# Stores and reloads moved from SyncE's DMA queue to GpSimd's, a spare buffer for one weight chunk, and another order at the first rows and the last stores

## The chip, the cores and the metric

One Trainium2 chip (trn2), one core, one launch. The metric is the device time of that launch in microseconds (us). The engines are named as in the profile: PE (TensorE matmul), PEld (its weight loads), DVE (VectorE), ACT (ScalarE), POOL (GpSimd) and SP (SyncE, which here only issues DMAs). Each engine runs its own instruction list in order; semaphores tie the lists together. A DMA is issued by one engine's list (its "queue") and runs on 16 shared DMA engines. If an issue has to wait for a semaphore, everything behind it in that list waits too.

## The reference, cut to what matters

```python
def reference(A_x, A_dft_seq_re, A_dft_seq_im, A_dft_hid_re, A_dft_hid_im, B_x, B_w1, B_b1, B_w2, B_b2):
    x = A_x                                  # (1, 2048, 640), f32
    xn = _layernorm(x, axis=-1)
    # fourier half: y = Cr @ (xn @ Wr^T) - Ci @ (xn @ Wi^T), sequence 2048, hidden 640
    # MLP half:     gelu(xn @ w1 + b1) @ w2 + b2, w1 (640, 1536), w2 (1536, 640)
    return x + _A_ref(xn, A_dft_seq_re, A_dft_seq_im, A_dft_hid_re, A_dft_hid_im) + _B_ref(xn, B_w1, B_b1, B_w2, B_b2)
```

B_x is not used: both halves work on the same normalized rows.

## The kernel before

All matmuls are f32 by way of a split: each operand is kept as a rounded high part (`high`, ACT, L182) and the rest (`low`, DVE, L185), and a product is three matmuls, high by high, high by low, low by high (`product`, L307 to L309; `hidden`, L325).

The 2048 rows are four blocks of 512 (t = 0 to 3). The first third of the time is the MLP half, the rest the Fourier half; only the first third, the beginning and the end bear on the change.

**Beginning.** Four chunks of 128 rows of block 0 are loaded, two by SP and two by ACT (`load_x`, L204). PE runs 26 matmuls on zeros meanwhile (`NWARM`, L662). DVE takes mean and variance of each chunk (`ln_stats`, L211 and L212), `ln_scale` makes the factors, and the normalized chunks are transposed on PE.

**Block 0** goes through 12 hidden units (`hidden`, then `gelu`, then `output`) while `background(i)` brings in other rows: block 2's (`rows_b`) and block 1's (`row`) are normalized in place (L227), stored to a DRAM tensor `xs` (`put_rows`, L232) and loaded back in a layout for transposing (`load_z`, L262: four loads, `z_b` for block 2, `row` for block 1). DVE transposes these (L266), and ACT and DVE split them into the moving operands of the next stage.

**Blocks 1 and 2** run together in `pair(k)`, k = 0 to 5: each pair makes two hidden units of both blocks out of seven products (`window`) in place of eight. The units of block 1 are used at once; those of block 2 are stored to DRAM (`keep`, `gs`, L851) out of a tile `ab` of which there are two. The weights of a pair are made from two w1 chunks by `make_pieces`; chunks are loaded by `load_w1` (L285, four DMAs each) into three buffers `w1r`, the next two when the two of a pair are used up (after "Cl" and "Dl"). `w2r`, also three buffers, holds w2 chunks in block 0's stage, later other tiles. Beside the pairs, called by `beside_pair(k, at)` at numbered points of a pair (in the order 2, 5, 6, 3, 7, 4):

- `finish`: ACT adds the bias to an output bank, DVE transposes it (L384), POOL adds it to `xo` (L386); then `store_sums` writes `xo` to DRAM (`ys`, L864, three stores).
- `by_chunks` copies 512 rows of `xs` to `xn` in DRAM (L860).
- `prep_w(j, 0..2)`: the DFT matrices of the hidden axis are combined, split into the staging tile `wst` (which lies where `xo` was, so it waits for the `ys` stores) and other small tiles, and stored (`wit`, L438).

After the pairs block 2's units are loaded back (`load_unit`, L931) for its outputs; block 3's rows are normalized, stored, loaded back (`z`) and transposed in `between(p)`; block 3 then runs like block 0.

**Fourier half.** The DFT along the sequence, with combined forms of both matrices; its last products are transposed on DVE, added and stored (`store`, L1152; last lines L1581 to L1591).

Order of the work: `manual_schedule`, so each engine's list is in the order of the calls. In the kernel before SP issues all DMAs but the first rows, the first two w1 chunks and some of the last stores, which ACT issues.

Of the kernel before, what the change touches and what calls it, by code (L numbers as in the profile page):

```python
# [10 lines left out]
F32 = mybir.dt.float32  # L11
# [4 lines left out]
P = 128  # L16
Q = 4
B = 32
EPS = 1e-5
NWARM = 26  # L20
# [5 lines left out]
def kernel(  # L26
# [204 lines left out]
    def put_rows(c):  # L231
        nc.sync.dma_start(xs[c * P : (c + 1) * P], xt[c])  # L232
# [25 lines left out]
    def load_z(z, t):  # L258

        v = rows_of(xs, t)  # L260
        for q in range(Q):
            nc.sync.dma_start(z[q * B : (q + 1) * B], v[:, :, q * DQ : (q + 1) * DQ])  # L262
# [13 lines left out]
    def load_w1(i, eng=nc.sync):  # L276
# [4 lines left out]
        t = early.tile([P, ND, P], F32, tag="w1r", bufs=3, name=f"w1r{i}")  # L281
# [126 lines left out]
    def put_w(w, j, main, odd=None, negative=False):  # L408
# [28 lines left out]
        for t, c0, c1 in parts:  # L437
            nc.sync.dma_start(wits[w][j][:, :, c0:c1], t.bitcast(F32))  # L438
# [209 lines left out]
    warm = early.tile([P, TB], F32R, tag="w1r", bufs=3, name="warm")  # L648
    for c in range(NC):
        load_x(c, (nc.sync, nc.scalar)[c % 2])  # L650
# [3 lines left out]
    nc.vector.tensor_copy(warm, zeros)  # L654

    nc.scalar.activation(eps[:, 1:2], eps[:, 0:1], AF.Sqrt)
    load_w1(0, nc.scalar)
    load_w1(1, nc.scalar)

    wacc = bank(5)  # L660
    for k in range(NWARM):
        nc.tensor.matmul(wacc, warm[:, :P], warm, start=True, stop=True)  # L662
# [19 lines left out]
    for c in range(NC):  # L682
        ln_stats(c)

    last = NC - 1
    nc.vector.tensor_scalar(MV[:, last, 5:6], MV[:, last, 0:1], -1.0, None, op0=ALU.mult)
    ln_scale(NC)
# [4 lines left out]
        bias=MV[:, last, 5:6],  # L692
    )
    nc.scalar.activation(xp[:, last], xp[:, last], AF.Copy, scale=MV[:, last, 3:4])
    for c in (0, 1, last, 2):
# [114 lines left out]

    def make_pieces(k, *what):
# [6 lines left out]
        for w in what:  # L818
# [14 lines left out]
            if w in ("Cl", "Dl"):  # L833
                load_w1(n + 3 + (w == "Dl"))
# [15 lines left out]
    def keep(g, a):  # L850
        nc.sync.dma_start(gs[g % NF], a)  # L851
# [10 lines left out]
    def store_sums(t):  # L862
        for k, (c0, c1) in enumerate(YCOLS):
            nc.sync.dma_start(ys[k][t], xo[t][:, :, c0:c1])  # L864
# [5 lines left out]
    def beside_pair(k, at):  # L870
# [20 lines left out]
        if at == 6:  # L891
# [3 lines left out]
            turn_w(1, j)  # L895
        if at == 3:
            if k == 1:
                A["wst"] = zo_tile("wst", (P, NB * DQ), F32R)
            prep_w(j, 0)
# [6 lines left out]
        if at == 7:  # L906
            prep_w(j, 1)
            if k == LASTK:
                A["gs"] = place("xab3", (P, 5, TB), F32)
                for i in range(3, 6):  # L910
                    load_unit(i)
                prep_w(j, 2)
        if k < LASTK and at == 4:
            prep_w(j, 2)
# [708 lines left out]
```

## Time and profile before

| | us |
|---|---|
| runs | 886.62, 885.71, 883.77; median 885.71 |
| the profiled execution's own time | 888.06 |
| its span | 886.0 |
| PE busy (3718 matmuls) | 856.2 (97%) |
| DVE busy | 684.9 (77%) |
| ACT busy | 364.4 (41%) |
| POOL busy (22 instructions) | 22.8 (3%) |
| DMA: SP's queue, share of 16 engines | 70.5% |
| mean granted clock of PE | 0.989 |

How to read it: a line of a view names the kernel's line (L308), the engine, the operation, and out<-in by tile names. In brackets behind a timeline line stands the idle time of that engine just before the instruction, and what ended it. "SPq" and "ACTq" are DMA issues; the time of a DMA itself runs from its issue to its landing. The granted clock is the share of full speed that PE was given. A DMA share is the time that packets took, as a share of the time of all 16 DMA engines.

What the issues on SP cost and how long the transfers take to land, from the tile and DMA views (median ns of an issue; median us from issue to landing): xs stores 392, 4.8; z_b loads 481, 6.0; ys stores 524, 6.2; wit stores 504, 3.7; gs stores 452, 3.7.

### The profile page before, as it was taken

To read this page: it belongs to the slowest core of one execution; us is meant where nothing else is said; L and a number is where in the kernel's file an instruction comes from. 1 tells how busy PE (TensorE), PEld (TensorE's weight loads), DVE (VectorE), ACT (ScalarE), POOL (GpSimd) and SP (SyncE) were. 2 spreads that over 40 slices of the span, in tenths; PEclk is the share of its full clock that TensorE was granted. 3 is DMA by queue.
4 is the path that set the end of the run, shared out by engine and by line. 5 is a ranking of instruction groups with operands and counts; after the bars stand their busy time and mean duration, and the time that the engine had idled before them with its cause. 6 is when DMAs were issued, how large, how long until landed. Compare 5 with 4: busy or idle time off the path is not lost.

```text
span 886.0 us, 10517 instructions
## 1 busy us (share of the span) xinstructions
PE 856.2 (97%) x3718; PEld 701.0 (79%) x3718; DVE 684.9 (77%) x892; ACT 364.4 (41%) x520; POOL 22.8 (3%) x22
## 2 busy tenths in 40 slices
PE   8998979999889999999999999999999999999997
PEld 6886857878668788888888888888888888888885
DVE  6866957775674568898989888888977988886586
ACT  5554555554424455543343434332232423323241
POOL 0000011000030300000000000000000000000000
PEclk9998999999999999999999999999999999999999
DMA  6986448998989697896865259946475779904364
GB/s 178 308 228 162 95 102 217 282 277 265 293 250 199 162 365 281 150 182 161 196 141 161 56 149 325 249 95 178 114 178 189 226 210 217 333 18 172 119 179 88
DMA packets 228547, 171.76 MB, mean 194 GB/s; under 512 B 83728, under 2 KB 198416, under 8 KB 227856
## 3 DMA queue, kind: packets, MB, share of 16 engines
q1 hardware_dynamic: 222544, 169.13, 70.5%
q10 hardware_dynamic: 5952, 1.97, 0.9%
q8 instruction: 29, 0.48, 0.2%
q14 instruction: 22, 0.18, 0.1%
HBM read 124.92 MB, written 51.38 MB: 199 GB/s over the span
## 4 chain that ended last, share of the span: by engine, by line
PE 74%; DMA 12%; DVE 6%; SPq 3%; ACT 2%; issue 1%; POOL 1%; DVEq 0%; ACTq 0%; POOLq 0%
PE banks L308 23%; PE banks L307 23%; PE banks L309 23%; PE banks L325 5%; DMA gs<-ab 2%; DMA w1r<-in_B_w_dram 1%; DMA xs<-row 1%; DMA row<-in_A_x_dram 1%; DMA wit<-wst 1%; DVE hs L185 1%; DMA xn<-xs 1%; SPq L285 1%; PE banks L662 1%; SPq L398 1%; DMA ys<-xo 1%
## 5 line engine op out<-in xcount | busy, mean ns | idle before, releaser
L308 PE MATMUL banks<-as,xab 128*128 128x512 f32 x407 | 158.5, 389 | 0.0
L309 PE MATMUL banks<-as,xab 128*128 128x512 f32 x407 | 158.4, 389 | 0.0
L307 PE MATMUL banks<-as,xab 128*128 128x512 f32 x407 | 158.4, 389 | 0.0
L182 ACT ACTIVATE as<-r 128x1024 fp32r<-128x1024 f32 x80 | 85.0, 1062 | 173.3 <-PE banks L309 148.5
L185 DVE TENSOR_TENSOR as<-r,as 128x1024 fp32r<-128x1024 f32 x80 | 97.2, 1216 | 38.8 <-ACT as L182 38.8
L308 PEld LDWEIGHTS banks<-as,xab 128*128 128x128 f32 x407 | 76.4, 188 | 16.4 <-DVE as L185 0.6
L307 PEld LDWEIGHTS banks<-as,xab 128*128 128x128 f32 x407 | 76.4, 188 | 16.0
L309 PEld LDWEIGHTS banks<-as,xab 128*128 128x128 f32 x407 | 76.4, 188 | 15.7
L307 PE MATMUL banks<-as,xc 128*128 128x512 f32 x224 | 87.1, 389 | 0.0
L308 PE MATMUL banks<-as,xc 128*128 128x512 f32 x224 | 87.1, 389 | 0.0
L309 PE MATMUL banks<-as,xc 128*128 128x512 f32 x224 | 87.1, 389 | 0.0
L182 ACT ACTIVATE as<-rt 128x1024 fp32r<-128x1024 f32 x32 | 34.0, 1062 | 69.8 <-PE banks L309 57.9
L185 DVE TENSOR_TENSOR hs<-ab,hs 128x512 fp32r<-128x512 f32 x36 | 26.3, 732 | 39.8 <-ACT hs L182 39.4
L325 PE MATMUL banks<-xt,xab 128*128 128x512 f32 x240 | 56.8, 390 | 0.2 <-ACT xt L182 0.2
L307 PE MATMUL banks<-hs,xc 128*128 128x512 f32 x120 | 47.9, 399 | 6.8 <-DVE ot L384 6.5
L325 PEld LDWEIGHTS banks<-xt,xab 128*128 128x128 f32 x240 | 44.7, 188 | 10.3 <-ACT xt L182 1.3
L308 PE MATMUL banks<-hs,xc 128*128 128x512 f32 x120 | 47.3, 394 | 2.0 <-DVE hs L185 2.0
L307 PEld LDWEIGHTS banks<-as,xc 128*128 128x128 f32 x224 | 42.0, 188 | 8.8
L309 PEld LDWEIGHTS banks<-as,xc 128*128 128x128 f32 x224 | 42.0, 188 | 8.7
L308 PEld LDWEIGHTS banks<-as,xc 128*128 128x128 f32 x224 | 42.0, 188 | 8.7
L309 PE MATMUL banks<-hs,xc 128*128 128x512 f32 x120 | 47.0, 391 | 0.0
L185 DVE TENSOR_TENSOR as<-rt,as 128x1024 fp32r<-128x1024 f32 x32 | 38.8, 1212 | 5.3 <-ACT as L182 5.3
(200 smaller groups left out, 1605.8 us busy)
## 6 DMA issues: line engine op xcount, KB each, us to landing
raw<-in_A_dft_seq_re_dram SPq DMA_DIRECT2D x64, 256.0 KB, 5.6
raw<-in_A_dft_seq_im_dram SPq DMA_DIRECT2D x64, 256.0 KB, 5.2
w1r<-in_B_w_dram SPq DMA_DIRECT2D x136, 80.0 KB, 3.1
wit<-wst SPq DMA_DIRECT2D x15, 384.0 KB, 5.0
ws<-wit SPq DMA_DIRECT2D x15, 384.0 KB, 5.4
xn<-xs SPq DMA_DIRECT2D x4, 1280.0 KB, 8.4
wit<-wst SPq DMA_DIRECT2D x20, 256.0 KB, 3.2
forms_ab<-xab SPq DMA_DIRECT2D x4, 1280.0 KB, 7.9
```

Source lines behind the costliest of these rows:

```text
L182: nc.scalar.activation(h, s, AF.Copy)
L185: nc.vector.tensor_tensor(l, s, h.bitcast(F32), op=ALU.subtract)
L285: eng.dma_start(t[q * B : (q + 1) * B], v[q, :, :, f0 : f0 + P])
L307: nc.tensor.matmul(acc, wh, mh, start=first, stop=False, skip_group_check=goes_on)
L308: nc.tensor.matmul(acc, wh, ml, start=False, stop=False, skip_group_check=goes_on)
L309: nc.tensor.matmul(acc, wl, mh, start=False, stop=last, skip_group_check=goes_on)
L325: nc.tensor.matmul(acc, W1[i][:, a, j * P : (j + 1) * P], XT[j][:, b], start=n == 0, stop=n == len(steps) - 1)
L398: nc.sync.dma_start(t[q * B : (q + 1) * B], v[:, :, s0 : s0 + B])
L662: nc.tensor.matmul(wacc, warm[:, :P], warm, start=True, stop=True)
```

## The change

1. `put_rows`, `load_z`, `put_w`'s stores, `keep` and `store_sums` issue on POOL's queue instead of SP's.
2. w1 chunk NF + 5 = 17 takes a `w2r` buffer, and the loads of chunks 15 to 20 are called earlier (`NEXT_W1`): 15 by pair 0's pieces "Cl", 16 and 17 by its "Dl", 18 and 19 by pair 1's, 20 by pair 2's; from 21 on as before.
3. `prep_w` of the first hidden chunk: step 0 at point 7 of pair 1 (was 3), step 1 at point 4 (was 7), step 2 at point 5 of pair 2 (was 4 of pair 1). The others keep their points.
4. First rows: SP loads all four chunks, chunk 1 first; ACT works out chunk 1's mean and variance, DVE those of the other three; chunks are transposed in the order 0, 2, 1, 3. 19 instead of 26 matmuls on zeros, in three tiles that are the three `w1r` buffers, so that the loads of w1 chunks 0, 1 and 2, now all on SP, wait for matmul 4, 8 and 19.
5. Last stores: the add `v1` of the last stage moves behind the split of the next operand (`form`); the four stores of three pieces are shared out between SP and ACT in another way, and the very last piece is transposed, added and stored whole and not in two halves.

```diff
...
 Q = 4
 B = 32
 EPS = 1e-5
-NWARM = 26
+NWARM = 19
+NGATE = 4
 TAIL = 4
 PADL = 8
 
...
             put_rows(c)
 
     def put_rows(c):
-        nc.sync.dma_start(xs[c * P : (c + 1) * P], xt[c])
+        nc.gpsimd.dma_start(xs[c * P : (c + 1) * P], xt[c])
 
     def ln_apply_chunked(dst, c):
 
...
 
         v = rows_of(xs, t)
         for q in range(Q):
-            nc.sync.dma_start(z[q * B : (q + 1) * B], v[:, :, q * DQ : (q + 1) * DQ])
+            nc.gpsimd.dma_start(z[q * B : (q + 1) * B], v[:, :, q * DQ : (q + 1) * DQ])
 
     def transpose_z(key, z, j):
         zt[key] = mr.tile([P, TB], F32, tag="zt", bufs=2, name=f"zt{key}")
...
         if i >= 3 * NF:
             return
         f0 = (i % NF if i < 2 * NF else AGAIN[i - 2 * NF]) * P
-        t = early.tile([P, ND, P], F32, tag="w1r", bufs=3, name=f"w1r{i}")
+        t = early.tile([P, ND, P], F32, tag="w2r" if i == NF + 5 else "w1r", bufs=3, name=f"w1r{i}")
         w1r[i] = t
         v = w1.rearrange("(q c i) f -> q i c f", q=Q, i=B)
         for q in range(Q):
...
             nc.scalar.activation(h, odd, AF.Copy, scale=-1.0)
             nc.vector.scalar_tensor_tensor(l, odd, -1.0, h.bitcast(F32), op0=ALU.mult, op1=ALU.subtract)
         for t, c0, c1 in parts:
-            nc.sync.dma_start(wits[w][j][:, :, c0:c1], t.bitcast(F32))
+            nc.gpsimd.dma_start(wits[w][j][:, :, c0:c1], t.bitcast(F32))
 
     def prep_w(j, k):
 
...
 
     zeros = rows.tile([P, TB], F32, tag="yt", bufs=2, name="zeros")
 
-    warm = early.tile([P, TB], F32R, tag="w1r", bufs=3, name="warm")
-    for c in range(NC):
-        load_x(c, (nc.sync, nc.scalar)[c % 2])
+    warms = [early.tile([P, TB], F32R, tag="w1r", bufs=3, name=f"warm{k}") for k in range(3)]
+
+    for c in (1, 0, 2, 3):
+        load_x(c)
     nc.gpsimd.memset(eps, EPS)
     make_identity(nc, ident)
     nc.vector.memset(zeros, 0.0)
-    nc.vector.tensor_copy(warm, zeros)
+    for warm in warms:
+        nc.vector.tensor_copy(warm, zeros)
 
     nc.scalar.activation(eps[:, 1:2], eps[:, 0:1], AF.Sqrt)
-    load_w1(0, nc.scalar)
-    load_w1(1, nc.scalar)
+    load_w1(0)
+    load_w1(1)
 
     wacc = bank(5)
     for k in range(NWARM):
+        warm = warms[min(k // NGATE, 2)]
         nc.tensor.matmul(wacc, warm[:, :P], warm, start=True, stop=True)
     load_w1(2)
     load_w2(0)
...
         for j in range(ND):
             nc.tensor.transpose(tacc[j][:, c * P : (c + 1) * P], xp[:, c, j * P : (j + 1) * P], ident)
 
-    for c in range(NC):
-        ln_stats(c)
-
-    last = NC - 1
-    nc.vector.tensor_scalar(MV[:, last, 5:6], MV[:, last, 0:1], -1.0, None, op0=ALU.mult)
-    ln_scale(NC)
+
+    last = 1
+    m = MV[:, last]
+    scratch = mr.tile([P, 2 * TB], F32, tag="hs", bufs=3, name="scratch")[:, :D]
+    nc.scalar.activation(scratch, xt[last], AF.Copy, accum_out=m[:, 4:5])
+    nc.scalar.activation(m[:, 5:6], m[:, 4:5], AF.Copy, scale=-1.0 / D)
     nc.scalar.activation(
         chunked(xp[:, last]),
         xt[last].rearrange("p (q c i) -> p q c i", q=Q, i=B),
         AF.Identity,
-        bias=MV[:, last, 5:6],
+        bias=m[:, 5:6],
     )
+    nc.scalar.activation(scratch, xp[:, last], AF.Square, accum_out=m[:, 2:3])
+    nc.scalar.activation(m[:, 1:2], m[:, 2:3], AF.Copy, scale=1.0 / D)
+    nc.scalar.activation(m[:, 0:1], m[:, 5:6], AF.Copy, scale=-1.0)
+    for c in (0, 2, 3):
+        ln_stats(c)
+    ln_scale(NC)
     nc.scalar.activation(xp[:, last], xp[:, last], AF.Copy, scale=MV[:, last, 3:4])
-    for c in (0, 1, last, 2):
+    for c in (0, 2, last, 3):
         if c != last:
             ln_apply_chunked(xp[:, c], c)
         transpose_x(c)
...
             WP[key] = w[:, lo : lo + 2 * n * P].rearrange("p (a b) -> p a b", a=2)
             lo += 2 * n * P
 
+
+    NEXT_W1 = (
+        {"Cl": (15,), "Dl": (16, 17)},
+        {"Cl": (18,), "Dl": (19,)},
+        {"Cl": (20,)},
+        {"Cl": (21,), "Dl": (22,)},
+        {"Cl": (23,), "Dl": (24,)},
+        {"Cl": (25,), "Dl": (26,)},
+    )
+
     def make_pieces(k, *what):
         if k >= NF // 2:
             return
...
                 high(dst[:, 0], src)
             else:
                 low(dst[:, 1], src, dst[:, 0])
-            if w in ("Cl", "Dl"):
-                load_w1(n + 3 + (w == "Dl"))
+            for i in NEXT_W1[k].get(w, ()):
+                load_w1(i)
 
     def window(acc, key, col, form, first, odd=None):
 
...
             output(g, (e,))
 
     def keep(g, a):
-        nc.sync.dma_start(gs[g % NF], a)
+        nc.gpsimd.dma_start(gs[g % NF], a)
 
     def finish(t, *es, home=None):
 
...
 
     def store_sums(t):
         for k, (c0, c1) in enumerate(YCOLS):
-            nc.sync.dma_start(ys[k][t], xo[t][:, :, c0:c1])
+            nc.gpsimd.dma_start(ys[k][t], xo[t][:, :, c0:c1])
 
     in_zt = {"home": mr, "tag": "zt"}
 
...
                 by_chunks(k - 1)
             turn_w(0, j)
             turn_w(1, j)
+
+        steps = {7: (0,), 4: (1,)} if k == 1 else {3: (0,), 7: (1, 2) if k == LASTK else (1,), 4: () if k == LASTK else (2,)}
+        if k == 2 and at == 5:
+            prep_w(0, 2)
         if at == 3:
-            if k == 1:
-                A["wst"] = zo_tile("wst", (P, NB * DQ), F32R)
-            prep_w(j, 0)
             if j + 1 < ND:
                 load_w(0, j + 1)
                 load_w(1, j + 1)
             if k == LASTK:
                 load_x(12)
                 load_x(13)
-        if at == 7:
-            prep_w(j, 1)
-            if k == LASTK:
-                A["gs"] = place("xab3", (P, 5, TB), F32)
-                for i in range(3, 6):
-                    load_unit(i)
-                prep_w(j, 2)
-        if k < LASTK and at == 4:
-            prep_w(j, 2)
+        if k == 1 and at == 7:
+            A["wst"] = zo_tile("wst", (P, NB * DQ), F32R)
+        for n in steps.get(at, ()):
+            prep_w(j, n)
+        if k == LASTK and at == 7:
+            A["gs"] = place("xab3", (P, 5, TB), F32)
+            for i in range(3, 6):
+                load_unit(i)
         if k == LASTK and at == 2:
             for i in range(3):
                 load_unit(i)
...
             for k in names:
                 nc.sync.dma_start(part_of(t, k), sums[t, k])
 
-    def store(t, src, c0, c1, both=False, n0=0, n1=NB):
+    def store(t, src, c0, c1, on_act=0):
 
         for q in range(Q):
-            (nc.scalar if both and q > 1 else nc.sync).dma_start(
-                rows_of(out, t)[:, n0:n1, q * DQ + c0 : q * DQ + c1], src[q * B : (q + 1) * B, n0:n1]
+            (nc.scalar if q >= Q - on_act else nc.sync).dma_start(
+                rows_of(out, t)[:, :, q * DQ + c0 : q * DQ + c1], src[q * B : (q + 1) * B]
             )
 
     def reload(lo, w, which="xab"):
...
             return f
 
         def out_b(k):
-            return lambda: store(tb, columns(k), 2 * k * B, 2 * (k + 1) * B, last and k == 1)
+            return lambda: store(tb, columns(k), 2 * k * B, 2 * (k + 1) * B, Q if last and k == 1 else 0)
 
         yb1, yb2 = in_two(0), in_two(1)
-        yb4 = to(yo[tb, 4], vs, f"yb4_{tb}", lambda: store(tb, yo[tb, 4], 4 * B, DQ, last))
+        yb4 = to(yo[tb, 4], vs, f"yb4_{tb}", lambda: store(tb, yo[tb, 4], 4 * B, DQ))
         f5s = [lambda u=u: f5(u) for u in range(2)] if not last else [lambda: None] * 2
         f6s = [lambda u=u: f6(u) for u in range(2)] if not last else [lambda: None] * 2
-        pre = {
-            17: [lambda: add(s(1, "v1"), s(1, "v1"), x_)],
-        }.get(n, [])
+        v1 = lambda: add(s(1, "v1"), s(1, "v1"), x_)
+        pre = [v1] if n == 17 and not last else []
         post = {
 
             0: [lambda: gather(1, tb, "v1", z_), lambda: gather(1, tb, "v", vs, op=ALU.subtract), f5s[0]],
...
             14: [lambda: add(s(1, "v2"), s(1, "v2"), z_), yb1],
             15: [yb1] if last else [load_yb(0)],
             16: [] if last else [load_yb(1)],
-            17: [yb2, yb2] if last else [yb1, yb2],
+            17: [v1, yb2, yb2] if last else [yb1, yb2],
             18: [yb4] if last else [yb2],
             19: [f6s[0]],
             20: [] if last else [f6s[1], yb4],
...
 
 
     t = blocks[-2][1]
-    y = yo[t]
-    add_turned(y[:, :, 2 * B : 3 * B], turned(bank(X), "yt_2"))
-    store(t, y[:, :, 2 * B : 3 * B], 2 * B, 3 * B, True)
-    yt = A["yt"]("yt_last")[:, 0].rearrange("p (n i) -> p n i", i=B)
-    d, a = y[:, :, 3 * B : 4 * B], bank(X + 1).rearrange("p (n i) -> p n i", i=B)
-    for n0 in (0, NB // 2):
-        rows_ = slice(n0, n0 + NB // 2)
-        nc.vector.transpose(yt[:, rows_], a[:, rows_])
-        add(d[:, rows_], d[:, rows_], yt[:, rows_])
-        store(t, d, 3 * B, 4 * B, True, n0, n0 + NB // 2)
+    for k, on_act in ((2, Q), (3, Q // 2)):
+        d = yo[t][:, :, k * B : (k + 1) * B]
+        add_turned(d, turned(bank(X + k - 2), f"yt_{k}"))
+        store(t, d, k * B, (k + 1) * B, on_act)
 
 
 # ---- launch: one core; inputs and outputs as the reference has them ----
```

## The prediction

> **What bounds the kernel now.** I read the page first (PE busy 97% of an 886.0 us span, so at most some 30 us are idle), then the windows of the span, then PE's waits, then the queue that the waits lead to. The windows (columns: stretch, busy PE, PEld, DVE, ACT, POOL with counts, granted clock, DMA share, GB/s):
>
> ```profile
> 0.00:13.22 13.22, 10.70 (x47) 8.55 (x47) 8.22 (x25) 4.62 (x8) 0.74 (x7) 1.00 0.56 174
> 13.22:74.50 61.28, 61.28 (x270) 50.30 (x270) 41.84 (x84) 32.29 (x48) 0.00 (x0) 1.00 0.91 252
> 74.50:82.20 7.70, 3.76 (x10) 2.54 (x9) 6.79 (x11) 5.14 (x10) 0.00 (x0) 0.74 0.45 118
> 82.20:117.70 35.50, 35.50 (x152) 29.17 (x151) 30.28 (x49) 19.22 (x33) 0.00 (x0) 0.96 0.51 111
> 117.70:145.00 27.30, 19.90 (x71) 14.59 (x70) 16.38 (x31) 13.16 (x26) 6.35 (x5) 0.87 0.51 129
> 145.00:296.00 151.00, 141.69 (x606) 113.84 (x605) 98.85 (x196) 74.96 (x147) 13.24 (x9) 0.99 0.90 248
> 296.00:879.40 583.40, 583.39 (x2571) 481.99 (x2569) 480.84 (x497) 215.01 (x253) 2.50 (x2) 1.00 0.68 185
> 879.40:886.00 6.60, 0.00 (x0) 0.00 (x0) 1.66 (x4) 0.00 (x0) 0.00 (x0) 0.83 0.44 73
> ```
>
> From 296 us to 879.4 us PE never stops, so nothing can be won there; all holes lie before 296 us and at the two ends. PE's waits name who fills them:
>
> ```profile
> PE banks L307 <- DVE ot L384: 6.5, 4, 3.4
> PE banks L325 <- ACT as L182: 3.9, 1, 3.9
> PE banks L308 <- DVE hs L185: 2.4, 3, 1.3
> PE banks L307 <- ACT hs L182: 2.3, 1, 2.3
> ```
>
> At full rate 15 matmuls take 3.40 us (0.227 each, from the chain). Spacing of starts beyond that, the slow matmuls after each hole included (0.42 to 0.43 us apart at 79 to 82, 131 to 136 and 266 to 269 us, where the clock is granted low), gives the losses: A at 74.5 us, 6.7; B at 117.7, 1.7; C at 124 to 136, 7.9; D at 141, 1.6; E at 186, 1.4; F at 232 to 245, 4.5; G at 261 to 269, 4.8; H at 287 to 295, 2.8. Sum 31.4 us. Behind them stands SP, which issues nearly every DMA in order:
>
> ```profile
> 58.59 2.38 SPq L232 DMA_DIRECT2D xs<-row  x4
> 65.19 1.91 SPq L262 DMA_DIRECT2D row<-xs  x4
> 119.94 3.69 SPq L285 DMA_DIRECT2D w1r<-in_B_w_dram  x8
> 123.99 12.74 SPq L864 DMA_DIRECT2D ys<-xo  x3
> 246.02 2.12 SPq L232 DMA_DIRECT2D xs<-row  x4
> ```
>
> ```profile
> 49.41 2.18 DVE L227 TENSOR_SCALAR row<-row,mv 128x640 f32<-128x640 f32 x4
> 73.39 1.30 DVE L266 STREAM_TRANSPOSE ztua<-row 128x512 f32<-128x512 f32 x2 [9.08 <-DMA row<-xs]
> 78.04 0.72 ACT L182 ACTIVATE as<-w1r 128x640 fp32r<-128x640 f32 x1
> 125.49 1.15 ACT L182 ACTIVATE w1f<-w1r 128x384 fp32r<-128x384 f32 x2 [4.12 <-DMA w1r<-in_B_w_dram]
> 187.20 0.69 ACT L344 ACTIVATE ab<-banks,b1c 128x512 f32<-128x512 f32 x1 [5.13 <-DMA gs<-ab]
> 261.37 1.30 DVE L266 STREAM_TRANSPOSE ztx<-z 128x512 f32<-128x512 f32 x2 [6.17 <-DMA z<-xs]
> ```
>
> In A the rows are normalized at 51.6 us, but their stores go out from 58.59, behind weight loads, and the reload lands at 73.4. In C, ACT waits for a w1 chunk that had no free buffer. In D to H the queue stands in waits for POOL or DVE (ys: 12.74 us) with loads behind them.
>
> **The change, step by step.** 89 DMAs go from SP to POOL's queue: 16 xs, 12 z, 12 gs, 9 ys, 40 wit. The trace has no DMA on POOL. Lower end of the price: the same DMAs on SP, 0.39 (xs), 0.48 (z), 0.52 us (ys). Upper end: POOL's own add of 128x512 takes 1.28 us, and if software there paid that for every 128 contiguous runs of a DMA, a z load (512 runs) would cost 5.1 and a ys store (2048) 20 us. I take 1.2 us whatever the runs, for on SP the ys issue with 16 times the runs of an xs issue costs only 0.13 us more, and POOL is nearly empty (22.8 us busy). Both ends stay for the range.
>
> A: the stores of block 2's rows start when DVE is done (about 39 to 40.5 us) and land some 4.4 us later; z_b loads take POOL from 46 to 51. Block 1's stores then follow at 50.8 to 55.6, land by 60 (4.4 us as for rows_b), its loads go at 60 to 65 and land near 69, as 8.2 us passed from first issue to landing before. ACT's `as` ends 5.4 us after that landing and PE wants it at 74.7, so the hole nearly closes. But DVE is 30.28 of 35.50 us busy in the next stretch, so PE gains no more than the landing does: 73.4 - 69 = 4.4. Lower end 0, upper 6.7.
>
> The Trainium skill (SBUF — State Buffer, "SBUF: two separate sides") says that while VectorE runs an instruction in a two-port mode, GpSimd cannot write the descriptors of its DMAs. No row here shows it. By it the four row stores would start after the last L227 (51.6) and not at 50.8, A would be 3.6, and the sum 0.8 us later.
>
> B: the first gs is ready at 111.7 (ACT L344), went out at 113.0 and landed at 117.1. With 1.2 us on POOL and the median landing of 3.7 it lands at 116.6: 0.5.
>
> C: chunk 17 gets a w2 buffer and is loaded with 15 and 16 near 100 us, so ACT's 4.12 us wait goes, and with it both holes and the slow matmuls behind them; 7.3 of 7.9, as the bias and transpose before PE's next output group (0.64 + 0.72) still have to fit.
>
> D: the staging tile `wst` waits for the ys stores. Moved one product later; POOL's adds end near 129 in the shortened run, three issues and 4.2 us landing give 137, some 2 to 3 us after ACT wants it. Queued behind it on ACT is the gelu of the next unit, for which PE has ten output groups (30 matmuls, 6.8 us) and 24 more matmuls (5.4): the wait is covered, gain 1.3. Without that cover it would cost 3. On POOL the next gs stands behind the ys stores; same cover.
>
> E: gs leaves the ring where it stood behind the 1280 KB xn copy (9.09 us): 1.2. F: wit stores and row loads no longer take turns on SP; the load at 230.74 can go some 5 us earlier, DVE's 3.65 us wait goes: 3.0 of 4.5. G: rows are normalized earlier and stored at once, not at 246.02; z lands some 4 us earlier, and 2.6 us pass from it to PE: 3.0 of 4.8. H: the w1 loads no longer wait for ys on SP; 1.3 of 2.8, the rest being the block's own transposes and adds.
>
> Start: three row statistics on DVE in place of four (1.03 us each), the fourth on ACT beside them: 1.0. The w1 loads wait for warm matmuls; chunk 0 is issued by 5.5 us and lands (3.8 us, ACT's row) before ACT wants it near 9.6. If the rows, now issued by SP alone (0.43 each), land late: 0. Seven warm matmuls fewer end before the rows are ready, so they cost nothing. Lower end of the start: 0.5 lost.
>
> End: SP issued six stores after 879.82 and finished at 883.81. Now two per queue follow DVE (0.72 + 0.69 after 879.43, so 880.9 to 881.9) and land in 2.1 instead of 1.6: 1.4.
>
> Sum: 1.0 + 4.4 + 0.5 + 7.3 + 1.3 + 1.2 + 3.0 + 3.0 + 1.3 + 1.4 = 24.4 us. The profiled execution took 888.06 us (span 886.0 and 2.06 around it): 863.7. The runs shown have a median 2.35 us lower: 861.3, say 861.5.
>
> **Rivals.** (1) The reloads land no earlier. For: the DMA share is 0.91 from 13 to 74 us and 0.90 from 145 to 296. Against: 0.45 in A's hole itself. A, F and G stay (10.4 us): 872. The Trainium skill (DMA: Bandwidth & Descriptors, "Rules for kernel authors") says that spreading DMAs over queues saves issue time only, which is this rival; the trace shows both a full engine share and a blocked queue.
>
> (2) Slower: POOL pays by runs. At 0.65 us for 128 runs (half the upper end) z takes 2.6 and ys 10.4 us each. Block 1's stores wait for POOL until 56, the reload lands at 79: A grows by 5. Three ys hold the next gs until 160, and PE, covered to about 145, stalls some 20 in place of C and D's 9.5. With the other gains left: 892; at the full price near 940. It decides from about 0.55 us for 128 runs. Against: SP's issue hardly depends on runs.
>
> (3) The queue was only hiding waits for buffers, and they return as SP waits for DVE (L285 has such waits: 9.0 and 7.6 us): 885. Against: C's buffer is added.
>
> **How the numbers follow.** Forecast 0.60, own range 853 to 870; rival 1 0.20 (868 to 880); rival 2 0.15; rival 3 0.05. About 0.3% (2.7 us) can be told from no change here. So faster 0.80, same 0.05, slower 0.15. The low end is all 31.4 us, start and end won, 885.7 - 33.8 = 852; the high end, 882, takes in rival 1 and leaves rival 2 out.
>
> **What would show it.** A: no DVE wait over 5 us before ztua and the clock near 1.00 at 75 to 85 us. C: no ACT wait for w1r. POOL: the time between its DMAs near 1.2 us, ys included. E: no ACT L344 wait for gs. End: the last issue about 2.5 us after the last matmul. Wrong if PE waits behind POOL's queue near 130 us, or ztua starts after 73 us.

## The result and the profile after

The changed kernel takes 880.68 us (median of 7 runs, 879.65 to 883.43), the kernel before in the same session 885.17 us: ratio 0.9961, 95% interval 0.9942 to 0.998. It is faster, but by 4.5 us where 24 were forecast. The profiled execution took 883.43 us, its span is 881.6 us.

First the windows of the changed kernel from 75 to 296 us, cut at the same events as those of before (columns: stretch, busy PE, PEld, DVE, ACT, POOL with counts, granted clock, DMA share, GB/s).

```profile
75.10:83.60 8.50, 5.29 (x18) 3.75 (x17) 7.69 (x12) 5.90 (x11) 0.00 (x0) 0.80 0.26 72
83.60:118.00 34.40, 33.37 (x147) 27.12 (x145) 30.09 (x50) 20.05 (x34) 1.13 (x2) 1.00 0.51 113
118.00:147.00 29.00, 24.63 (x98) 18.75 (x98) 18.42 (x37) 14.40 (x30) 13.80 (x15) 0.94 0.75 214
147.00:296.00 149.00, 139.99 (x590) 113.67 (x589) 96.42 (x189) 71.53 (x140) 48.11 (x65) 0.95 0.84 244
```

PE's hole at 75 us is still there. From 118 to 147 PE has gained: 4.4 us are idle in place of 7.4 (27.30 - 19.90). From 147 to 296 us it still stands idle for 9.0 us (149.00 - 139.99), nearly as much as before (9.3), at a lower clock (0.95, was 0.99). The longest waits of PE are these:

```profile
PE banks L309 <- DVE hs L186: 6.1, 2, 5.9
PE banks L326 <- ACT as L183: 3.2, 1, 3.2
```

A single wait of 5.9 us stands at the top, longer than any before (3.9). To place them, the same count of losses as in the prediction (spacing of matmul starts beyond 0.227 us), in us. The last three columns are runs of the next section.

| place | before | forecast | after | chunk 17 alone | queues and ends alone | best version |
|---|---|---|---|---|---|---|
| A, 75 us (with one at 95) | 6.7 | 2.3 | 5.9 | 7.0 | 6.7 | 6.2 |
| B and C, 118 to 136 | 9.8 | 2.0 | 2.5 | 5.0 | 7.5 | 2.9 |
| D, 141 | 1.6 | 0.3 | 4.5 | 4.7 | 3.8 | 1.5 |
| E, 186 | 1.4 | 0.2 | 0 | 0 | 0 | 0 |
| F, 225 to 245 | 4.5 | 1.5 | 1.1 | 1.0 | 0.8 | 0.6 |
| G, 248 to 270 | 4.9 | 1.9 | 14.3 | 3.3 | 13.4 | 4.3 |
| H, 277 to 295 | 2.6 | 1.3 | 0 | 2.0 | 0 | 1.1 |
| sum | 31.5 | 9.5 | 28.3 | 23.0 | 32.2 | 16.6 |

So G is where the time went. POOL's queue tells how (timeline: start, duration, instruction; in brackets the idle time before it and what ended it):

```profile
52.86 2.48 POOL L233 DMA_DIRECT2D xs<-row  x4 [1.58 <-DVE row L228]
63.80 2.61 POOL L263 DMA_DIRECT2D row<-xs  x4 [8.46 <-DMA xs<-row]
...
130.11 3.43 POOL L884 DMA_DIRECT2D ys<-xo  x3
133.24 1.39 POOL L871 DMA_DIRECT2D gs<-ab  x2
...
236.24 3.38 POOL L387 TENSOR_TENSOR xab<-xab,ot 128x512 f32<-128x512 f32 x2 [16.60 <-DMA xab<-in_A_x_dram]
239.57 2.15 POOL L233 DMA_DIRECT2D xs<-row  x4
247.00 2.61 POOL L263 DMA_DIRECT2D z<-xs  x4 [5.28 <-DMA xs<-row]
249.63 3.70 POOL L387 TENSOR_TENSOR xab<-xab,ot 128x512 f32<-128x512 f32 x3
```

and the engines that depend on it:

```profile
139.97 1.12 ACT L183 ACTIVATE wst<-row 128x256 fp32r<-128x256 f32 x4 [7.10 <-DMA gs<-ab]
...
232.04 2.18 DVE L228 TENSOR_SCALAR row<-row,mv 128x640 f32<-128x640 f32 x4
...
246.45 0.55 SPq L880 DMA_DIRECT2D xn<-xs  x1
250.94 0.72 DVE L385 STREAM_TRANSPOSE ot<-banks 128x512 f32<-128x512 f32 x1 [10.03 <-POOL xab L387]
260.02 1.30 DVE L267 STREAM_TRANSPOSE ztx<-z 128x512 f32<-128x512 f32 x2 [5.40 <-DMA z<-xs]
```

Read the 236 to 261 us stretch as one story. DVE had block 3's rows normalized from 232.0 to 234.2 us, 9.7 us earlier than before, as hoped. But POOL is one list in order. Its two adds (L387) waited for a load of x until 236.2, so the row stores behind them left only at 239.6. The z loads behind those waited for the stores to land until 247.0, and three more adds stood behind the z loads. DVE's `ot` wants the buffer that such an add frees: it waited 10.0 us, and PE, fed by DVE, stood for 5.9. Then z itself landed only at 260.0: the 1280 KB `xn` copy had gone out on SP just ahead of it. Before, the copy went out behind z:

```profile
241.69 2.18 DVE L227 TENSOR_SCALAR row<-row,mv 128x640 f32<-128x640 f32 x4
...
252.85 1.91 SPq L262 DMA_DIRECT2D z<-xs  x4
254.81 2.11 SPq L285 DMA_DIRECT2D w1r<-in_B_w_dram  x4
256.97 0.59 SPq L860 DMA_DIRECT2D xn<-xs  x1
```

Counted from DVE's first normalized row, the stores began after 7.5 us (before: 4.3), the z loads after 15.0 (before: 11.2), and z had landed after 28.0 (before: 19.7). In absolute time z landed 1.4 us sooner than before (260.02 to 261.37). PE, which had won time at the earlier places, came to G 9.7 us ahead of the kernel before (the same matmul starts at 234.88 and at 244.53 us) and left it 0.5 us ahead (265.41 and 265.92). So nearly all that had been won up to there was given back here.

### The profile page after: what moved, and what is told of

It is laid out like the page before. It is cut to its first block, busy times and chain, and to the rows that moved or that the text cites. A ratio compares the mean times of both kernels' runs of the same rounds, so it can differ in the third digit from the quotient of the medians.

```text
span 881.6 us, 10526 instructions
## 1 busy us (share of the span) xinstructions
PE 853.3 (97%) x3711; PEld 700.4 (79%) x3711; DVE 682.6 (77%) x888; ACT 366.7 (42%) x527; POOL 79.2 (9%) x111
## 4 chain that ended last, share of the span: by engine, by line
PE 80%; DMA 8%; DVE 5%; SPq 2%; issue 2%; POOL 1%; ACT 1%; DVEq 0%; ACTq 0%; POOLq 0%
PE banks L309 25%; PE banks L310 25%; PE banks L308 25%; PE banks L326 5%; DMA w1r<-in_B_w_dram 3%; DMA xs<-row 2%; DMA row<-in_A_x_dram 1%; DVE xab L186 1%; SPq L286 1%; SPq L399 1%; DMA row<-xs 1%; DMA rows_b<-in_A_x_dram 1%; PE banks L666 1%; DVE st L212 1%; DVE w1f L186 0%
## 5 line engine op out<-in xcount | busy, mean ns | idle before, releaser
L308 PE MATMUL banks<-hs,xc 128*128 128x512 f32 x120 | 46.9, 391 | 1.3 <-DVE ot L385 1.3
L309 PE MATMUL banks<-hs,xc 128*128 128x512 f32 x120 | 46.8, 390 | 0.2 <-DVE hs L186 0.2
L310 PE MATMUL banks<-hs,xc 128*128 128x512 f32 x120 | 46.7, 390 | 0.0
```

The costliest lines, as they stand in the source:

```text
L308: nc.tensor.matmul(acc, wh, mh, start=first, stop=False, skip_group_check=goes_on)
L309: nc.tensor.matmul(acc, wh, ml, start=False, stop=False, skip_group_check=goes_on)
L310: nc.tensor.matmul(acc, wl, mh, start=False, stop=last, skip_group_check=goes_on)
```

## The experiments

All time ratios are against the kernel before, run on the same chip in the same session. Diffs are against the changed kernel unless said otherwise.

| run | median us | ratio | 95% interval |
|---|---|---|---|
| block 3 on SP | 874.28 | 0.9863 | 0.9834 to 0.9892 |
| xn copy later | 877.07 | 0.9892 | 0.9867 to 0.9917 |
| staging tile at another place | 882.51 | 0.9963 | 0.9945 to 0.9981 |
| first rows as before | 880.79 | 0.9925 | 0.9896 to 0.9954 |
| block 3 on SP, xn later | 875.54 | 0.988 | 0.9844 to 0.9917 |
| block 3 and gs on SP, staging tile | 876.50 | 0.9899 | 0.9875 to 0.9923 |
| block 3 on SP, block 1's stores on ACT | 875.05 | 0.9879 | 0.9849 to 0.9909 |
| kernel before with chunk 17 alone | 880.32 | 0.994 | 0.9917 to 0.9963 |
| block 3 and ys of block 1 on SP | 874.93 | 0.987 | 0.9847 to 0.9893 |
| the same, xn later | 878.29 | 0.9912 | 0.989 to 0.9935 |
| queues and ends without chunk 17 | 886.57 | 0.9998 | 0.9983 to 1.0013 |
| block 3 and ys of block 1 on SP, first rows as before | 876.24 | 0.989 | 0.9868 to 0.9911 |
| block 3 on SP, ys of block 1 on ACT | 874.49 | 0.9863 | 0.984 to 0.9886 |
| block 3 on SP, first ys store early | 875.31 | 0.9872 | 0.9848 to 0.9896 |
| both of these (best) | 871.70 | 0.9837 | 0.981 to 0.9864 |

### Which part of the change earns the time

The kernel before, with the chunk's edit alone:

```diff
-        t = early.tile([P, ND, P], F32, tag="w1r", bufs=3, name=f"w1r{i}")
+        t = early.tile([P, ND, P], F32, tag="w2r" if i == NF + 5 else "w1r", bufs=3, name=f"w1r{i}")
...
-            if w in ("Cl", "Dl"):
-                load_w1(n + 3 + (w == "Dl"))
+            for i in NEXT_W1[k].get(w, ()):
+                load_w1(i)
```

> The kernel before with one part of the change alone: w1 chunk 17 in a w2 buffer, and the w1 loads asked for by the new table. All DMAs stay on SP, and the ends are as before. Theory: the chunk's wait (4.1 us on ACT) made the larger part of the loss from 117 to 136 us (9.6 us); with the buffer alone 5 us of it go, so 881 to 882 where the kernel before takes 886.6. Rival 1: the loads still stand behind the ys stores on SP, chunk 17 lands no earlier, and the gain is under 1 us (886). Rival 2: the chunk takes a w2 buffer that the next w2 load wants, and a new wait for w2 takes the gain.

And the changed kernel with that edit undone, all else kept:

> The changed kernel without its chunk-17 part (w1 chunk 17 in a w1 buffer, loads asked for as before): the moves to POOL's queue and the two ends alone. The run of the chunk alone was 5.4 us faster than the kernel before, more than the whole change (4.5). Theory A: the rest of the change is worth about nothing (its gains in A, E, F and H are given back in G and D), and the parts add: this run is at 885 to 887, no faster than the kernel before. Theory B: the two parts overlap, as both shorten the stretch from 117 to 136 us, so the moves alone gain 2 to 4 us: 882 to 884.

The chunk alone gave 5.4 us (885.74 to 880.32), the whole change 4.5, and everything but the chunk nothing (0.9998). The table of losses shows the rest as a swap: queues and ends alone win 2.3 us in B and C, 1.4 in E, 3.7 in F and 2.6 in H, and lose 2.2 in D and 8.5 in G.

The chunk gave more than its own hole, and that was not expected. B, C and D together fell only from 11.4 to 9.7 us, but E and most of F went too. SP's queue shows why. In the kernel before:

```profile
177.37 0.59 SPq L860 DMA_DIRECT2D xn<-xs  x1
178.05 0.54 SPq L851 DMA_DIRECT2D gs<-ab  x1
...
230.74 0.97 SPq L204 DMA_DIRECT2D row<-in_A_x_dram  x2
```

With the chunk alone:

```profile
170.99 0.59 SPq L869 DMA_DIRECT2D xn<-xs  x1
175.14 0.32 SPq L860 DMA_DIRECT2D gs<-ab  x1
...
225.87 0.92 SPq L204 DMA_DIRECT2D row<-in_A_x_dram  x2
```

The copy is 6.4 us earlier although PE has lost only 1.4 us less by then (16.7 in place of 18.1 in A to D), so SP is 5 us less behind its work; gs no longer stands right behind the 1280 KB copy, and the row loads are 4.9 us earlier. The forecast gave these gains to POOL's queue. Taking one wait away on SP brought them as well, so they could not be had twice.

### G: the order on POOL, and what goes out early

```diff
-        nc.gpsimd.dma_start(xs[c * P : (c + 1) * P], xt[c])
+        (nc.sync if c >= 3 * NC else nc.gpsimd).dma_start(xs[c * P : (c + 1) * P], xt[c])
...
-            nc.gpsimd.dma_start(z[q * B : (q + 1) * B], v[:, :, q * DQ : (q + 1) * DQ])
+            (nc.sync if t == 3 else nc.gpsimd).dma_start(z[q * B : (q + 1) * B], v[:, :, q * DQ : (q + 1) * DQ])
```

> As the changed kernel, but the row stores and the z reloads of block 3 are issued by SP again; everything else stays on POOL. Theory: the 14.3 us that PE loses between 248 and 269 us come from POOL's order. The z reloads stand on POOL waiting for their stores, and the adds that the next `ot` needs stand behind them. Then the wait of `ot` for POOL (10.0 us) and the PE hole of 5.9 us near 255 go, z lands well before 260, PE loses at most 5 us in that stretch, and the time falls by some 9 us to 870 to 873. Rival: the z loads are late because they share the DMA engines with the 1280 KB xn copy. Then z still lands near 260, the second hole (2.4 us and the slow matmuls behind it) stays, and only the first goes: 874 to 876. Rival 2, that POOL's place has nothing to do with it: no change, 880.

The ratio falls from 0.9961 to 0.9863, about 8.7 us of 886.6. In this run's timeline:

```profile
233.39 2.31 SPq L233 DMA_DIRECT2D xs<-row  x4
239.96 1.91 SPq L263 DMA_DIRECT2D z<-xs  x4
...
233.49 8.97 POOL L387 TENSOR_TENSOR xab<-xab,ot 128x512 f32<-128x512 f32 x5 [15.91 <-DMA xab<-in_A_x_dram]
242.41 3.43 POOL L884 DMA_DIRECT2D ys<-xab  x3
...
248.37 1.31 DVE L267 STREAM_TRANSPOSE ztx<-z 128x512 f32<-128x512 f32 x2 [5.36 <-DMA z<-xs]
...
251.67 0.74 ACT L183 ACTIVATE as<-w1r 128x640 fp32r<-128x640 f32 x1 [1.92 <-DMA w1r<-in_B_w_dram]
```

The five adds run in one piece, the wait of `ot` for POOL is gone, and z lands 11.7 us earlier. G falls from 14.3 to 6.9 us; at most 5 were expected, and 870 to 873 us. The run does not tell the theory from the copy as its rival, for on SP the z loads (239.96) also leave ahead of the copy again (243.88). Then only the `xn` copy was moved behind z:

```diff
-        if p == 5:
+        if p == 9:
             by_chunks(3)
```

> As the changed kernel, but the 1280 KB xn copy of block 3 is asked for four products later, so that it no longer goes out at 246 us just ahead of the z loads. Theory (POOL's order): the first hole, 5.9 us of `ot` waiting for POOL, stays, since the adds still stand behind the waiting reloads; the z loads, issued at 247.0 to 249.6, may land some 4 us earlier than 260, and then only the second hole shrinks: 877 to 880. Rival (contention with the copy makes the whole stall): both holes shrink by most of their 14 us: 868 to 871. If the copy is then itself late for the w1 and row work that reads xn, a new wait on the copy shows, and the time rises.

877.07, G 8.5. The first hole stayed, as the theory of POOL's order says:

```profile
PE banks L309 <- DVE hs L186: 5.8, 2, 5.4
```

Of the second, some 8 us, about 3 were left. So both mechanisms are in G: moving the copy away gave 5.8 us, moving block 3 to SP, which undoes both, gave 7.4. No run took away the order on POOL alone, so their shares are not separated. What is left with block 3 on SP is ACT's wait for a w1 chunk. Both diffs together were to remove it:

> As the run with block 3 on SP, and the 1280 KB xn copy is asked for four products later as well. In the run with block 3 on SP alone the z reloads land at 248.4, but PE still loses 6.85 us between 249 and 260, as ACT waits for a w1 chunk (1.9 and 2.3 us) that SP issues behind the copy and that lands with it. Theory (what is left there is the copy in front of the w1 loads): the loss falls to 3 us or less and the time by 3 to 4 us against that run, to about 871 where the kernel before takes 886.6. Rival (the w1 chunks wait for their buffers, not for the copy): ACT still waits for w1r and the loss stays at 6 to 7: 874.

That failed: 875.54, G 9.1. ACT no longer waited for w1, but the row stores were slower in this run (8.2 us from their first issue to the z loads, where the run with block 3 on SP had 6.6), and the last z load took 9.9 us to land, beside 16 w1 loads that now followed it at once and the ys stores of block 1. The line at 242.41 above shows these: POOL sends 1280 KB that nobody waits for as soon as its adds end. In the kernel before SP reached them only at 275.4 us, with the chunk alone at 267.4. So the next runs held them back, first on SP:

```diff
-            nc.gpsimd.dma_start(ys[k][t], xo[t][:, :, c0:c1])
+            (nc.sync if t == 1 else nc.gpsimd).dma_start(ys[k][t], xo[t][:, :, c0:c1])
```

> As the run with block 3 on SP, and block 1's ys stores (1.25 MB) are issued by SP again as well. With them on POOL they go out at 242.4 us, as soon as POOL's adds end, beside the z reloads and the w1 chunks that PE waits for; in the kernel before SP reached them only near 268. Theory: a transfer that nobody waits for, let out early, takes the DMA engines from the ones that PE waits for. With it back on SP, the w1 loads land in 3 to 6 us in place of up to 12 and PE loses about 3.3 us between 249 and 262 (as the run with chunk 17 alone) in place of 6.9 to 8.0: 4 us faster than the run with block 3 on SP, near 870. Rival: the 1280 KB xn copy alone is what the w1 chunk waits behind; then the hole stays at 6 to 8 us: 874.

And with the diff of the xn copy as well:

> As the run with block 3 and ys of block 1 on SP, with the xn copy four products later. Theory (what counts is how many bytes that nobody waits for go out beside z and w1): only z and w1 are left between 240 and 250 us, so PE loses at most 2 us there: about 1 to 2 us faster than the run without the later copy, 868 to 869. Rival: as with the later copy before, nothing is gained, since w1 chunks then go out in its place; same time as the run without it.

G fell to 3.5 us as foretold, and to 4.2 where at most 2 were foretold, but the time did not fall: SP stands in these stores for 7 us near 266, DVE then waits 5.7 and 6.5 us for the w1 chunk behind them, and H is back at 2.2 and 6.0. With the later copy the run was even slower (878.29). On ACT's queue, late in the program, they block neither:

```diff
-            nc.gpsimd.dma_start(ys[k][t], xo[t][:, :, c0:c1])
+            (nc.scalar if t == 1 else nc.gpsimd).dma_start(ys[k][t], xo[t][:, :, c0:c1])
```

> As the run with block 3 on SP, with block 1's ys stores issued by ACT, at their late place in the program. Theory: they then neither start early beside z and w1 (POOL: 242 us, a loss of 6.9 to 8.0 in G) nor hold the w1 loads on SP (2.2 to 6.0 us near 280): G 3.5 and H 0, so 3 to 4 us faster than the run with block 3 on SP, 870 to 871 (ratio 0.983). Rival 1: ACT pays for the issue in front of the gelus that PE waits for, and a new hole of 2 to 3 us stands near 265: 874. Rival 2: the landing of z and w1 differs from chip to chip by more than this: no difference.

The wait for w1 and H's hole were small (0.6 us each), yet G was 6.9 and the time that of block 3 on SP, not the 870 to 871 foretold: in this profile the row stores took 8.3 us from issue to the z loads in place of 6.6, so z came late by itself. Over all runs with block 3 on SP, G is 6.9 to 9.1 (mean 8.0, five runs) where these stores go out early and 3.5 to 6.9 (mean 4.6, five runs, one of them this one, one the best version below) where they are held back. The early stores' cost is seen in the traces; the times of single runs do not separate it.

### D: what the staging tile waits for

```diff
-        steps = {7: (0,), 4: (1,)} if k == 1 else {3: (0,), 7: (1, 2) if k == LASTK else (1,), 4: () if k == LASTK else (2,)}
+        steps = {4: (0, 1)} if k == 1 else {3: (0,), 7: (1, 2) if k == LASTK else (1,), 4: () if k == LASTK else (2,)}
...
-        if k == 1 and at == 7:
+        if k == 1 and at == 4:
```

> As the changed kernel, but the staging tile of the weight products is made, and the first weight piece prepared, at the product where the second one is (three products later than in the changed kernel). Theory: the 4.45 us that PE loses near 140 us are ACT's wait of 7.1 us in front of the staging tile for the ys stores, with the next gelus queued behind it; by the later place the ys stores have landed, PE loses 0.5 us or less there, and the time falls by 3 to 4 us to 877. Rival: ACT waits for something else (the next weight pieces or the gs round trip) and the hole only moves to the later place: 880 to 882.

No gain (882.51), D 5.0: the rival. The wait only changed hands. Then gs 2 and 3 went to SP as well, on top of block 3 on SP (the "1.5 MB" of the text is 1280 KB):

```diff
-        nc.gpsimd.dma_start(gs[g % NF], a)
+        (nc.sync if g % NF in (2, 3) else nc.gpsimd).dma_start(gs[g % NF], a)
```

> As the run with block 3 on SP, with the staging tile made at the place of the second weight piece (which alone only moved the hole), and gs units 2 and 3 issued on SP. Theory: the hole near 140 us has two waits, both on POOL's queue: the staging tile waits for the ys stores, and ACT's next gelu for the gs store that stands behind the three ys stores in the same queue and lands 7 us after its issue. With gs on SP it lands in about 4 us, by 137 or 138, ACT's wait for gs (7.7 us) shrinks to 4 or less, and PE loses at most 1.5 us near 140 in place of 3.8 to 5.0: about 3 us faster than the run with block 3 on SP. Rival: gs is late since the ys stores fill the DMA engines (1.5 MB), whatever queue it is on; then it lands near 140 again and nothing is gained.

ACT in the run with the staging tile moved, and then with gs on SP too:

```profile
141.18 0.69 ACT L345 ACTIVATE ab<-banks,b1c 128x512 f32<-128x512 f32 x1 [7.74 <-DMA gs<-ab]
```

```profile
135.32 0.69 ACT L345 ACTIVATE ab<-banks,b1c 128x512 f32<-128x512 f32 x1 [3.30 <-PE banks L310]
...
139.90 1.43 ACT L183 ACTIVATE wst<-row 128x256 fp32r<-128x256 f32 x5 [3.23 <-DMA ys<-xo]
```

The gelu no longer waits for gs (first theory right), but the staging tile still waits for ys until 139.9, the next gelu stands behind it, D is 4.9 and nothing is gained (876.50). In the changed kernel the profile had put the wait at 139.97 down to gs, which landed last; the earlier cause, ys, showed only when gs was out of the way. What remained was to bring ys home sooner, again on top of block 3 on SP, with the staging tile at its place:

```diff
-    def store_sums(t):
-        for k, (c0, c1) in enumerate(YCOLS):
+    def store_sums(t, ks=(0, 1, 2)):
+        for k, (c0, c1) in ((k, YCOLS[k]) for k in ks):
...
-                finish(0, 2, home=in_zt)
+                store_sums(0, (0,)), finish(0, 2, home=in_zt)
...
-                store_sums(0)
+                store_sums(0, (1, 2))
```

> As the run with block 3 on SP, with the first of block 0's three ys stores (512 of 1280 KB) issued some 8 us earlier, as soon as POOL has added its two columns. Theory: D (3.8 to 5.0 us near 140) is set by the landing of the ys stores, 7 to 8 us after POOL's issues at 130; with 40% of the bytes gone by then the rest lands near 136 in place of 138 to 140, the staging tile's wait on ACT shrinks by 2 to 3 us, and D falls to 1 to 2 us: 2 to 3 us faster, 871 to 872. Rival: D is set by ACT and DVE, which prepare the weight pieces in front of the gelu, whenever ys lands; then D stays near 4: 874.

```profile
121.34 1.15 POOL L884 DMA_DIRECT2D ys<-xo  x1 [0.30 <-POOL xo L387]
129.94 2.27 POOL L884 DMA_DIRECT2D ys<-xo  x2
...
136.98 1.13 ACT L183 ACTIVATE wst<-row 128x256 fp32r<-128x256 f32 x4 [4.27 <-DMA gs<-ab]
```

D fell to 1.5 us here and in the best version: the landing of ys sets D. (The gs store behind it leaves sooner in these runs as well, but in the run above, with gs on SP, an earlier gs alone did not help.) The time did not fall (875.31): in this profile A was about 1 us larger, and z landed only 0.5 us sooner, so G was 7.8.

### A: a queue of its own

On top of block 3 on SP:

```diff
-        (nc.sync if c >= 3 * NC else nc.gpsimd).dma_start(xs[c * P : (c + 1) * P], xt[c])
+        (nc.sync if c >= 3 * NC else nc.scalar if NC <= c < 2 * NC else nc.gpsimd).dma_start(xs[c * P : (c + 1) * P], xt[c])
```

> As the run with block 3 on SP, with the row stores of block 1 issued by ACT in place of POOL. In that run they go out at 52 us behind the z_b loads of block 2 in POOL's queue and land at 63.0, 8.6 us after the last issue. Theory (transfers of one queue run in order, so the stores wait for the z_b loads ahead of them): on a queue of their own they land by 59 to 60, the reloads go out 3 us earlier, land near 69.5 in place of 72, and A's loss falls from 4.7 to about 2: 2 to 3 us faster. Rival (the DMA engines are full from 54 to 62 us, share 1.05): the stores still land near 63 or the z_b loads give up what the stores win, the reload lands near 72 as before, and the time stays within 1 us.

The rival held: nothing was gained. With block 3 on SP the stores began at 51.99 us and the reloads behind them went out at 63.04; with the stores on ACT:

```profile
53.16 3.04 ACTq L233 DMA_DIRECT2D xs<-row  x4
63.18 2.58 POOL L263 DMA_DIRECT2D row<-xs  x4 [11.33 <-DMA w2r<-in_B_w_dram]
...
54.00:58.00 4.00, 4.00 (x19) 3.34 (x18) 0.70 (x2) 1.76 (x2) 0.00 (x0) 1.00 1.04 236
```

The stores had a list to themselves. They began 1.2 us later, as this run's first real matmul came 1.4 us later, and the reloads followed after 10.0 us in place of 11.1, with the DMA engines full meanwhile (share 1.04). The profile names a w2 load as the last before the reloads; by the code these wait for the stores too. A stayed at 5.5 us, within 0.2 us of the run without this edit, and the time within 1 us. So a queue of its own saves at most about 1 us of eleven here and does not mend A. That the bytes hold A back is the likeliest reading, but no run took bytes away. The Trainium skill (DMA: Bandwidth & Descriptors, "Rules for kernel authors") says that DMAs spread over queues share the same engines and save issue time only; this run agrees in that A did not shrink (5.5 us). Over the 15 profiles that have these stores off SP, A is 5.4 to 9.3 us, mean 6.5, against 6.7 and 7.0 in the two with them on SP.

### The start

The first rows, warm-up and statistics of before (edit 4 of the change undone), first in the changed kernel:

```diff
-    for c in (1, 0, 2, 3):
-        load_x(c)
+    for c in range(NC):
+        load_x(c, (nc.sync, nc.scalar)[c % 2])
...
-    load_w1(0)
-    load_w1(1)
+    load_w1(0, nc.scalar)
+    load_w1(1, nc.scalar)
...
```

> As the changed kernel, but the first rows, the warm-up matmuls and the first statistics as in the kernel before (two queues for the rows, all statistics on DVE, one warm tile, 26 warm matmuls). Theory: the edit of the start costs some 0.7 us, as four rows issued on one queue land one after the other by 8.1 us and the first real matmul starts at 13.88 instead of 13.22 us: this kernel is 0.7 us faster than the changed one, 880.0, with DVE's waits for the first rows gone. Rival: the start as changed lets the later loads go sooner, and block A's w1 work gains from it what the start loses: no difference or up to 1 us slower.

and then on top of block 3 and ys of block 1 on SP:

> As the run with block 3 and ys of block 1 on SP, with the first rows, warm-up and first statistics as in the kernel before. In the runs so far the first real matmul began at 13.20 to 13.25 us with the old start (4 runs) and between 12.66 and 14.17 with the new one (7 runs, mean 13.4). Theory: the new start gains nothing, as one queue brings the rows later by what the statistics save: the same time within 1.5 us. Rival: the new start does gain its 1.0 us, and this run is 1 us slower with a first matmul near 13.2 against 12.7.

The first run's interval reaches from 0.9896 to 0.9954, so it may be faster than the changed kernel (0.9961), which that theory had at only 0.7 us; its profile shows no such gain (losses of 29.6 us, A at 8.5). The second is no faster than its partner (876.24 to 874.93). Neither settles it by its time. The first real matmul does: with the old start it comes at 13.15 to 13.25 us (four profiles; three when the text on record said four), with the new one at 12.54 to 14.17 (13 profiles, mean 13.27). The new start gained nothing on average and made the beginning uneven.

### The best version

Block 3 on SP, ys of block 1 on ACT and the first ys store of block 0 early:

> Both edits on the run with block 3 on SP: ys of block 1 on ACT, the first ys store of block 0 early. If both theories hold, 5 to 7 us faster than it: 867 to 869, ratio 0.980. If only one holds, 870 to 872; if neither, 874.

871.70 us, ratio 0.9837: faster than both kernels, though its interval overlaps that of block 3 on SP alone. Only some 2.6 of the 5 to 7 us came. PE's longest waits in it:

```profile
PE banks L326 <- ACT as L183: 3.8, 1, 3.8
PE banks L308 <- DVE ot L385: 2.7, 3, 1.7
```

A is now the largest hole. This version still moves most of the 89 DMAs to POOL and is 8.6 us faster than the chunk alone (871.70 to 880.32, from two sessions), so the moves do pay once the three places are mended.

## Why the prediction was wrong

The sign was right, the size was not. The time lies inside the full range (852 to 882), but that is luck: it lies outside the forecast's own range (853 to 870), and the high end was put there for rival 1, by which A, F and G stay as they are. F's gain came, and the loss in G became three times as large. Two of the signs named for A failed as well: DVE waited 7.54 us for the reload before ztua, which began at 73.30 us, and the clock from 75.1 to 83.6 us was 0.80. Term by term (gain forecast, gain measured in the traces):

- G, 3.0 forecast, -9.4 measured: this is the step that failed. The words "rows are normalized earlier and stored at once" took POOL as empty because it is 3% busy. The share said nothing about that place: five adds of block 1 are queued around these stores and reloads, and POOL's list is in order. I named what waits behind a waiting issue for the ys stores, and not for the z loads. The stores began 7.5 us after the first normalized row and not at once, and z landed 8.3 us later behind that row than before, not 4 us sooner: it stood behind POOL's adds and then behind the copy. And the sum added up places as if each stood alone. To keep what was won ahead of G, z had to come forward as far as PE did (9.7 us); it came 1.4.
- A, 4.4 forecast, 0.8 measured, and nothing on the mean of all runs. The sum let the stores land in 4.4 us, as rows_b's do. They took 8.5 after the last issue, in a stretch where the DMA share is 1.05 (54 to 62 us of the changed kernel). Rival 1 (the reloads land no earlier) was right for A; the share of 0.45 that I held against it belongs to the hole itself, after the transfers.
- D, 1.3 forecast, -2.9 measured. The cover was mis-sized: I counted ten output groups and 24 matmuls, 12.2 us, but only four groups are left there; PE had 8.2 us of work from 131 us on. The three ys stores took 4.9 to 7.7 us to land where 4.2 were assumed. That ys sets D is shown by the run with its first store early.
- B and C, 7.8 forecast, 7.3 measured; E, 1.2 and 1.4; F, 3.0 and 3.4: right in size; H, 1.3 and 2.6, was twice what was forecast. But the runs show a wrong share-out: the chunk's buffer alone gives 4.8 of B and C, all of E and 3.5 of F, while its D grows by 3.1.
- Start, 1.0 forecast, -0.7 in this profile and about 0 on average. The lower end, rows issued by SP alone landing late, is what happened.
- End, 1.4 forecast, 0.65 measured; from the start of the last matmul to the end it is 6.35 us, and 5.8 to 6.4 in the later runs, before 7.0. Right in kind.
- POOL's price, 1.2 us for every DMA, was too high for most (0.54 to 0.66 us for xs, z, gs; 1.22 for ys). Rival 2 fell: with 16 times the contiguous runs of an xs store, a ys store costs about twice as much. The sum did not hang on it. Rival 3 (885 us) comes near the time of queues and ends alone (886.57), but not by its mechanism: the waits came back behind POOL's list, in G and D, and not as waits of SP for DVE.

By the table, the losses fell by 3.2 us; start and end cancel, about 1.2 us lie in small spacings that the table leaves out, and that makes the 4.4 us by which the span fell.

## What to carry to other kernels

Before work is moved to a queue that looks idle, list that engine's instructions at each place where the new ones land: an issue that waits holds up every add behind it, and a share of 3% says nothing of the one place that matters. A queue that is blocked also holds back transfers that nobody needs yet; let loose, they can take bandwidth from those that PE waits for (G lost 8.0 us on average with the stores early, 4.6 with them held back), so ask of each moved transfer what it will run beside. And where two edits cure the same lateness, try each alone: here one buffer for one weight chunk was worth the whole change. And do not add up holes one by one: a gain ahead of a transfer that PE waits for is kept only if that transfer comes forward as well.

## What the runs showed of the hardware

- A DMA issued on POOL took 0.54 us (median; xs store, 128 contiguous runs; the first of a group up to 0.87), 0.66 (z load, 512 runs), 1.22 (ys store, 2048 runs).
- Beside DVE's L228 the first of four row stores took 0.86 to 0.87 us on POOL and all four 2.46 to 2.48 (three groups in the changed kernel, one of them beside the rows of 51.95 to 54.14 us). Block 3's four, issued while DVE ran other instructions, took 0.56 and 2.15. The rule weighed in the prediction (the Trainium skill, SBUF — State Buffer, "SBUF: two separate sides") did not hold the stores back to the last of the rows: they started 0.91 us after DVE began these four rows. Whether the extra 0.3 us is its effect stays open, for a gs store behind the ys stores took 0.85 us too, with no DVE instruction beside it.
- What stands ahead of a load in the DMA engines shows in its landing, even when it came by another queue: z took 9.3 to 9.4 us (median) in the four profiles where POOL issued it just behind SP's 1280 KB xn copy, and 5.2 to 5.7 in the others, where it went ahead of the copy.
- The landing of the same stores varied from run to run: from the row stores' first issue to the z loads 6.6 to 7.0 us in seven profiles with block 3 on SP, 7.6 to 8.3 in three, which was as much as some of the effects looked for.
